# One pool of eight PSUM banks, finer words and a new order behind the fifth pair, in a Mamba-2 scan with a low-rank mixer

## The chip, the cores and the metric

The kernel runs on one core of one Trainium2 chip. The metric is device microseconds of one execution, the median over the runs. Engine names are those of the profile: PE is TensorE (PEld its weight loads), DVE is VectorE, ACT is ScalarE, POOL is GpSimd, SP is SyncE, which issues the DMAs here.

## What is computed

First a Mamba-2 scan over batch 4, 8 heads, 768 positions, head size 32 and state size 16, in chunks of 32; then a mixer on its output, laid out as x of shape (4, 768, 256):

```python
# scan, per chunk c, with cum = cumsum(log a) inside the chunk
L = exp(cum[:, None] - cum[None, :]) * causal
y = ((C B^T) * L) x + (C state) * exp(cum)[:, None]
state = exp(sum(la)) * state + sum_j exp(cum[-1] - cum[j]) * B_j x_j^T
# mixer, per batch; U is 768 x 32, V is 32 x 768
h = x.T @ U @ V
u = x + h.T
out = u + relu(u @ w_ch1) @ w_ch2          # w_ch1 256 x 1024, w_ch2 1024 x 256
```

The mixer's weights come as float64 and are taken apart into float32 on the chip.

## The kernel before, in words

**Order.** The whole program is one list of words, PLAN (L36), that `follow` (L862) walks through: each word calls one helper with the numbers behind it, and the helper issues its instructions at once. Tiles are placed and semaphores set for that order; each engine runs its own instructions strictly in the order of the words, and so does SP its DMAs. Nothing is reordered later.

**Scan words.** The 12 pairs k are 4 batches of 3 pieces of 256 positions; pair k holds 8 chunks. `P` (`prep`, L460) multiplies B and C by their decays on DVE; `T` (`turning`, L472, two words for one pair) transposes them on PE and copies them with ACT to T and Cm; `g` (`gram`, L507) makes four PSUM tiles of scores in 32-row tiles of PE; `m` and `M` (`mask`, L520) mask two of them each on DVE; `n` (`intra`, L629) multiplies them with x in 64 small matmuls into the two y tiles; `s` (`state`, L537) makes the two A tiles of new state in 32 small matmuls; `u` (`update`, L552) adds them to the running state, four dependent DVE instructions (three in the last pair of a batch) and one POOL product; `i` and `j` (`inter`, L602) add the state's part to y, `j` behind a POOL marker copy that waits for the matmuls of `i` and `n` (`apart`, L577); `y` (`yout`, L644) copies the two y tiles out with ACT; `t` (`ytokening`, L653) transposes that into token order and copies it with ACT (batches 0, 1) or DVE. `L`, `B`, `X`, `b`, `x` load a pair (L190 to L214, five DMAs in all).

**Mixer words**, with b the batch, j the half of its 768 positions, m one of 8 column blocks, k one of 3 output chunks of 128: `p`, `q`, `a` form u = x + h^T (`project`, `parted`, `added`, L677 to L703; `a` takes two PSUM tiles and two DVE adds). For batch 0 `U` (L739) and four `d` words per chunk use plain fp32. For the other batches each operand is split into a near part, a far part and their join, all in the faster fp32r form: `S` (`split`, L718) makes the three parts of u (ACT, then DVE twice), `f` (L750) four products of 384 columns and a scaling on ACT, `e` (L756) two more into the same bank and the near part on ACT, `h` (L764) the far part on DVE and, for odd m, the join of the pair (`joined`, L713). `d` (`down`, L773) has six words per chunk of four products of 256 columns: near, near, far, far, join, join, with an ACT scaling behind the fourth; the last one adds a product, DVE adds the token tile and SP sends 128 KB to the output.

**Weights.** `w`, `W`, `Z`, `z` load the float64 words; `c` (`convert`, L807, four steps each) makes fp32 of them with ACT and DVE, `R` (`refined`, L835) the three parts.

**PSUM.** `bank` (L143) gives a tile under a tag; the tags w, x, z, y have two banks each (L131). f and U use x and z in turn by m, g takes both of x and z, s both of w, transposes w, y tiles y; d takes x, z or y.

```python
    BANKS = {"w": 2, "x": 2, "z": 2, "y": 2}

    def bank(tag, *dims):
        t = psum.tile([P, *dims], FP32, tag=tag, name=tag, bufs=BANKS[tag])
        return t
```

Of the kernel before, what the change touches and what calls it, by code (L numbers as in the profile page):

```python
# [10 lines left out]
FP32 = mybir.dt.float32  # L11
# [12 lines left out]
ALU = mybir.AluOpType  # L24
# [10 lines left out]
    'b0.0 b0.1 b0.2 x0.0 x0.1 b1.0 b1.1 b1.2 ')  # L35
PLAN = (  # L36
# [37 lines left out]


@with_exitstack
def kernel(
# [27 lines left out]
    nc = tc.nc  # L105
    P = 128
    NB, NH, S, D = x.shape
# [11 lines left out]
    NQ = NM // 2  # L119
# [8 lines left out]
    psum = ctx.enter_context(  # L128
        tc.tile_pool(name="psum", bufs=1, space=bass.MemoryType.PSUM))

    BANKS = {"w": 2, "x": 2, "z": 2, "y": 2}  # L131

    def idle(t, n):

# [6 lines left out]
            n -= m  # L141

    def bank(tag, *dims):  # L143
        t = psum.tile([P, *dims], FP32, tag=tag, name=tag, bufs=BANKS[tag])
        return t

    ctx.enter_context(tc.manual_schedule())

    class Kept:
# [23 lines left out]
        out=a_sb,  # L173
# [11 lines left out]
    def begin(**kwargs):  # L185
        op = nc.sync.dma_start(**kwargs)
        if until:
            hold(op, until.pop())
# [32 lines left out]
    w1all = mix.tile([P, NQ, NCB, W], FP32, tag="u", name="w1f", bufs=1)  # L221
    w1f = [w1all[:, c] for c in range(NQ)]
    w2 = [const.tile([P, NM, DM], FP32R, name=f"w2{i}") for i in range(2)]
    weights = []
    w2f, w2b = {}, {}

    def w2c(n, dtype):
        return (w2f if dtype == FP32 else w2b).setdefault(n, mix.tile(
            [P, 2, DM], dtype, tag=f"w2c{n}", name=f"w2c{n}", bufs=1))


    def words_of(dst):
        p, i, j = dst.shape
        t = raw.tile([P, 2 * WCOLS], INT32, tag="words", name="words", bufs=NWORDS)
        weights.append((dst, t[:p, :2 * i * j]))
        return t[:p, :2 * i * j]

    def each(parts, *index):
        return [part[index] for part in parts]

    def load_words(dst, src):

        p, i, j = dst.shape
        t = words_of(dst)
        begin(out=t.rearrange("p (i j) -> p i j", i=i), in_=src)

    U2, V2, w12, w22 = (w.bitcast(INT32) for w in (moe_U, moe_V, moe_w_ch1, moe_w_ch2))
# [4 lines left out]

    def load_v():
        own["UV"] = words_of(UV)
        for q in range(4):
            begin(out=own["UV"][ts(q, Q), 2 * NC * RK:], in_=V2[:, ts(q, 2 * NC * RK)])

# [3 lines left out]

    def load_w(n):
        if n < 2:
            if n == 0:
                own["w"] = words_of(w1f[0])
                weights.pop()
            dst, t = w1f[0][:, :, ts(n, P)], own["w"][:, ts(n, 2 * NCB * P)]
            weights.append((dst, t))
            begin(out=t.rearrange("p (i j) -> p i j", i=NCB),
                  in_=w13[:, :, ts(n, 2 * P)])  # L270
        elif n <= NQ:
            load_words(w1f[n - 1], w13[:, :, ts(n - 1, 2 * quarter)])
        else:
            m = 2 * (n - NQ - 1)
            load_words(w2c(n - NQ - 1, FP32), w22[m * P:(m + 2) * P].rearrange(
                "(m p) d -> p m d", p=P))

    def load(k):
# [273 lines left out]
    def update(k, c=0, n=2):  # L552
# [7 lines left out]
        for i in own:  # L560
# [4 lines left out]
            else:  # L565
# [2 lines left out]
                    op0=ALU.mult, op1=ALU.add)  # L568
            st["S", b] = new
            st["Sm", b, j + 1] = s["Sm"][:, i].rearrange("p s d -> p (s d)")  # L570
        sl = slice(own[0], own[-1] + 1)
        nc.gpsimd.tensor_tensor(  # L572
            out=s["Sm"][:, sl], in0=s["S"][:, sl].rearrange("p i (s d) -> p i s d", s=2),
            in1=own2[:, b, 4 * q + sl.start:4 * q + sl.stop, :, None].to_broadcast(
                [P, len(own), 2, D]), op=ALU.mult)

    def apart(k):  # L577

# [62 lines left out]
                            stop=True, skip_group_check=True)  # L641
                        behind.setdefault(k, []).append(product)

    def yout(k):  # L644
        b, q = pairs[k]
        if q == 0 and b:
            yT[b] = mix.tile([P, NCB, S], FP32, tag="yT", name="yT")
            ytok[b] = mix.tile([P, NC, DM], FP32, tag="ytok", name="ytok")
        yp = yT[b][:, :, ts(q, 2 * P)].rearrange("p g (c v i) -> p g c v i", c=2, v=2)
        for p in range(2):  # L650
            nc.scalar.copy(out=yp[:, :, :, p], in_=st[k]["y"][p])  # L651

    def ytokening(k, tag="w"):  # L653

# [17 lines left out]
    def mixer(b):  # L672
# [91 lines left out]
        def third(j, m):  # L764

            near, far, both = gs[j, m // 2]
            vector.scalar_tensor_tensor(
                out=far[:, m % 2], in0=gs["t", j, m], scalar=0.0,
                in1=near[:, m % 2].bitcast(FP32), op0=ALU.max, op1=ALU.subtract)
            if m % 2:  # L770
                joined(near, far, both)

        def down(j, k, n):  # L773

# [18 lines left out]
            if n == pieces - 1:  # L793
# [3 lines left out]
                nc.sync.dma_start(out=out[b, ts(c, P)], in_=o)  # L797

        us, gs, gT = {}, {}, {}
        return SimpleNamespace(p=project, q=parted, a=added, S=split, f=first, e=second, h=third,  # L800
                               d=down, U=plain)


# [46 lines left out]
    def ytokens_kept(k):  # L850
        next(turns["O", k])

    scans = dict(P=prep, T=turned, g=gram, s=state, m=lambda k: mask(k, (0, 1)),
                 M=lambda k: mask(k, (2, 3)), u=update, i=lambda k: inter(k, 0), n=intra,
                 j=lambda k: inter(k, 1), y=yout, t=ytokens, L=load, Q=lambda k, c: prep(k, c, 1),
                 O=ytokens_of, o=ytokens_kept,
                 V=lambda k, c, v: turn(k, c, 1, "wx"[v // 2], vector if v % 2 else None))
# [54 lines left out]
```

## Time and profile before

| what | value |
|---|---|
| median of 3 runs | 225.08 us (224.58 to 226.39) |
| profiled execution, its own time | 225.03 us |
| its span, first to last instruction | 223.3 us |
| busy in the span: PE, DVE, ACT, POOL | 215.1, 156.7, 114.5, 14.7 us |
| mean granted TensorE clock | 1.00 |
| one state word on PE (L546, 32 matmuls) | 0.38 us |
| one `i` or `j` (L616, 16 matmuls), one `n` (L638, 64) | 0.43, 0.79 us |
| four f products of 384 columns (L728) | 0.70 us |
| one `d` word in fp32r, four products of 256 columns | 0.47 us |
| masks, two on DVE | 0.75 us |
| far part, join on DVE | 0.55, 0.96 us |
| state update on DVE, three instructions | 0.91 us |

Durations are those of the rows; where several instructions of a kind follow each other their sum over the row is used, since they overlap a little. The time outside the span is 1.7 us.

### The profile page before, as it was taken

The numbers are of one execution on the slowest core, as the hardware profiler recorded it, in microseconds if no ns is written. First come the engines' busy times: TensorE is split into PE (matmuls) and PEld (weight loads), VectorE is DVE, ScalarE is ACT, GpSimd is POOL, SyncE is SP. The second block draws the span as 40 slices with busy tenths as digits, with TensorE's granted clock in tenths as the row PEclk, the third lists the DMA queues.
The fourth block names the chain that finished last, engine by engine and source line by source line (L and its number), as shares of the span: only waits on it lengthen the run. The fifth ranks groups of instructions, "written<-read, shape, count | busy, mean of one in ns | idle before, by whom it ended". The sixth has DMA issues, their size and how long they took to land.

```text
span 223.3 us, 7012 instructions
## 1 busy us (share of the span) xinstructions
PE 215.1 (96%) x3012; PEld 181.6 (81%) x3012; DVE 156.7 (70%) x330; ACT 114.5 (51%) x261; POOL 14.7 (7%) x37
## 2 busy tenths in 40 slices
PE   7989799999999999999999999999999999999993
PEld 4657565556678998987999898897998999999993
DVE  4786689899998857879627784849437965764921
ACT  2336766766993365425354533375237545655410
POOL 3021020013100000203001000100000000000000
PEclk9999999999999999999999999999999999999999
DMA  6987599777737014300003402000020000100111
GB/s 94 133 121 160 110 172 288 110 209 171 98 51 97 26 44 59 64 23 26 3 26 62 83 0 73 3 3 3 1 73 0 0 8 18 47 0 28 35 36 47
DMA packets 69518, 14.56 MB, mean 65 GB/s; under 512 B 63792, under 2 KB 67696, under 8 KB 69488
## 3 DMA queue, kind: packets, MB, share of 16 engines
q1 hardware_dynamic: 69488, 14.13, 31.8%
q8 instruction: 23, 0.38, 0.8%
q14 instruction: 7, 0.06, 0.1%
HBM read 10.98 MB, written 3.15 MB: 63 GB/s over the span
## 4 chain that ended last, share of the span: by engine, by line
PE 90%; DVE 4%; issue 2%; ACT 1%; DMA 1%; POOL 0%; DVEq 0%; POOLq 0%; ACTq 0%
PE x L728 31%; PE z L728 24%; PE y L728 12%; PE y L616 4%; PE y L638 4%; PE x L514 3%; PE w L483 3%; PE w L659 2%; PE w L546 2%; PE z L514 2%; PE w L682 1%; DMA a_sb<-in_a_dram 1%; DVE words L160 1%; PE w L138 1%; DVE S L160 1%
## 5 line engine op out<-in xcount | busy, mean ns | idle before, releaser
L160 DVE SCALAR_TENSOR_TENSOR words<-words 128x768 fp32r<-128x768 f32 (+6 forms) x44 | 34.6, 806 | 1.9 <-ACT words L419 0.6
L728 PE MATMUL z<-u,w 128*128 128x384 f32 x144 | 34.2, 351 | 0.0
L728 PE MATMUL x<-u,w 128*128 128x384 f32 x144 | 33.2, 347 | 0.0
L733 ACT ACTIVATE x<-x 128x384 f32<-128x384 f32 (+1 forms) x30 | 13.6, 452 | 25.1 <-PE x L728 24.1
L728 PEld LDWEIGHTS z<-u,w 128*128 128x128 f32 x144 | 24.5, 188 | 1.5 <-DVE words L160 0.2
L728 PEld LDWEIGHTS x<-u,w 128*128 128x128 f32 x144 | 24.0, 188 | 1.2 <-ACT x L733 0.6
L160 DVE SCALAR_TENSOR_TENSOR words<-x,words 128x384 fp32r<-128x384 f32 x24 | 13.2, 555 | 16.3 <-ACT words L762 13.6
L728 PE MATMUL x<-w2c,words 128*128 128x256 f32 x112 | 22.5, 338 | 0.0
L733 ACT ACTIVATE z<-z 128x384 f32<-128x384 f32 (+1 forms) x27 | 12.5, 463 | 14.2 <-PE z L728 13.8
L728 PEld LDWEIGHTS x<-w2c,words 128*128 128x128 f32 x112 | 18.3, 189 | 1.3
L728 PE MATMUL y<-w,words 128*128 128x256 f32 x144 | 18.9, 280 | 0.0
L728 PEld LDWEIGHTS y<-w,words 128*128 128x128 f32 x144 | 18.3, 188 | 0.4 <-DVE ytok L160 0.4
L160 DVE SCALAR_TENSOR_TENSOR words<-z,words 128x384 fp32r<-128x384 f32 x24 | 13.3, 552 | 5.6 <-ACT words L762 5.6
L762 ACT ACTIVATE words<-x 128x384 fp32r<-128x384 f32 x24 | 11.7, 490 | 6.3 <-PE x L728 6.2
L762 ACT ACTIVATE words<-z 128x384 fp32r<-128x384 f32 x24 | 11.6, 491 | 4.9 <-PE z L728 4.8
L651 ACT COPY yT<-y 128x256 f32<-128x256 f32 x24 | 7.9, 385 | 11.1 <-PE y L616 10.9
L572 POOL TENSOR_TENSOR Sm<-S,own 128x256 f32<-128x256 f32 (+1 forms) x12 | 7.7, 646 | 86.4 <-DVE S L160 57.0
L160 DVE SCALAR_TENSOR_TENSOR S<-S,kept,w 128x64 f32<-128x64 f32 x40 | 11.2, 280 | 2.7 <-PE w L546 1.0
L728 PE MATMUL x<-w,words 128*128 128x256 f32 x96 | 12.5, 281 | 0.0
L616 PE MATMUL y<-T,Sm 32*64 32x64 f32 x352 | 12.1, 239 | 0.3 <-POOL Sm L572 0.3
L638 PE MATMUL y<-M,x 64*32 64x64 f32 x768 | 11.0, 224 | 1.1 <-issue 1.0
L728 PEld LDWEIGHTS x<-w,words 128*128 128x128 f32 x96 | 11.9, 189 | 0.1
(153 smaller groups left out, 399.4 us busy)
## 6 DMA issues: line engine op xcount, KB each, us to landing
words<-in_moe_w_ch_dram SPq DMA_DIRECT2D x7, 512.0 KB, 6.4
x<-in_x_dram SPq DMA_DIRECT2D x24, 128.0 KB, 3.3
out_dram<-ytok SPq DMA_DIRECT2D x24, 128.0 KB, 1.7
bc<-in_B_dram SPq DMA_DIRECT2D x24, 64.0 KB, 3.1
bc<-in_C_dram SPq DMA_DIRECT2D x12, 128.0 KB, 3.1
words<-in_moe_w_ch_dram SPq DMA_DIRECT2D x2, 256.0 KB, 4.7
words<-in_moe_V_dram SPq DMA_DIRECT2D x4, 48.0 KB, 2.4
words<-in_moe_U_dram SPq DMA_DIRECT2D x1, 192.0 KB, 4.7
```

The source lines that it names most:

```text
L160: self.last = call(*args, **kwargs)
L483: nc.tensor.transpose(out=tp[:, i, v], in_=s["BC"][:, i, c + v].rearrange("p h n -> p (h n)"), identity=ident)
L514: nc.tensor.matmul(out=g[r][cols, c], lhsT=s["T"][rows, 0, c, cols], rhs=s["Cm"][rows, :, :, ts(2 * c + p, Q)].rearrange("r v t i -> r v i ...
L546: nc.tensor.matmul(out=s["A"][p][ts(r, Q), v], lhsT=s["BC"][half, 0, v, 2 * r:2 * r + 2].rearrange("p h n -> p (h n)"), rhs=x_sb[k][half, ...
L572: nc.gpsimd.tensor_tensor(out=s["Sm"][:, sl], in0=s["S"][:, sl].rearrange("p i (s d) -> p i s d", s=2), in1=own2[:, b, 4 * q + sl.start:4 ...
L616: product = nc.tensor.matmul(out=y[p][ts(r % 2, H), r // 2, c], lhsT=own[ts(r, Q)], rhs=s["T"][ts(r, Q), 1, :, ts(2 * c + p, Q)].rearrange ...
L638: product = nc.tensor.matmul(out=y[p][ts(i, Q), n, c], lhsT=x_sb[k][half, c, h], rhs=s["M"][half, h // 2, c, h % 2], start=fresh(k, p, [i] ...
L651: nc.scalar.copy(out=yp[:, :, :, p], in_=st[k]["y"][p])
L659: nc.tensor.transpose(out=t[:, c, g], in_=yT[b][:, g, ts(2 * q + c, P)], identity=ident)
L728: nc.tensor.matmul(out=t, lhsT=lhsT, rhs=rhs, start=start, stop=True, skip_group_check=True)
L733: nc.scalar.activation(t, t, AF.Copy, scale=1.0 + EPS)
L762: nc.scalar.activation(gs[j, m // 2][0][:, m % 2], t, AF.Relu, scale=NEAR)
```

## The change

Three things change. PSUM's eight banks become one pool under one tag, so that any tile takes any free bank; the names passed to `bank` stay as names only. The words u and y are cut in two (`u` by half pair, with the POOL product behind the second half; `y` by tile), and the join gets a word of its own, `J` (`fourth`), in place of a call inside `h`; the list of loaded weights becomes a dictionary, so that loads may come in another order. Behind u5 all words stand in a new order; in front of it the order is the same but for the cut words. Apart from the cut words and J both plans hold the same words.

Of the two plans, the lines that the text speaks of:

```diff
-    'x2.0 x2.1 b3.1 b3.2 W0 Z0 V2.0.2 V2.1.3 n1 i1 s2 g2 z0 x3.1 x3.0 W1 b4.0 j1 y1 P3 u2 m2 M2 T3 '
...
-    'w7 w8 U0.0.3 P6 U0.0.2 c6 U0.0.6 s5 c4 c4 U0.1.7 c6 U0.1.2 u5 R0 R2 U0.1.6 n4 s6 L7 i4 g5 c6 '
...
-    'd1.1.0.5 d1.1.2.4 d1.1.2.5 d1.1.1.4 d1.1.1.5 T10 g9 m9 T10 T11 T11 M9 i9 n9 g10 m10 M10 j9 y9 '
-    's11 u11 i10 g11 m11 M11 n10 f2.0.4 a2.1 f2.0.3 f2.0.2 e2.0.4 h2.0.4 e2.0.3 e2.0.2 f2.0.7 '
...
-    'e2.1.6 d2.1.0.0 e2.1.7 d2.1.2.0 d2.1.2.1 d2.1.2.2 h2.1.6 h2.1.7 d2.1.2.3 a3.0 S3.0 d2.1.0.1 '
...
-    'd3.1.0.2 d3.1.0.3 d3.1.2.4 d3.1.2.5 d3.1.0.4 d3.1.0.5 ')
+    'F1.0 j0 y0.0 y0.1 x2.0 x2.1 b3.1 b3.2 W0 Z0 V2.0.2 V2.1.3 n1 i1 s2 g2 z0 x3.1 x3.0 W1 b4.0 j1 '
+    'y1.0 y1.1 P3 u2.0 u2.1 m2 M2 T3 T3 O0.0 i2 c0 c1 c1 n2 g3 M3 c1 c1 j2 y2.0 y2.1 m3 t1 O2.1 s3 '
...
+    'c4 U0.1.7 c6 U0.1.2 u5.0 u5.1 R0 L8 T6 c7 U0.1.6 c7 U0.1.5 c7 i4 R3 g5 n4 m5 c6 T6 U0.0.5 M5 c8 '
+    'L7 c8 U0.0.4 c8 c9 c7 U0.1.4 U0.0.7 c9 c9 n5 c6 i5 j4 R5 P8 y4.1 y4.0 P7 g6 j5 m6 L10 y5.1 t4 '
+    'd0.1.0.0 T8 y5.0 d0.1.0.1 T8 c8 T7 T7 c9 M6 d0.1.0.2 d0.1.0.3 R1 R2 s6 n6 s7 s8 u6.0 u6.1 u7.0 '
+    't5 u7.1 u8.0 R2 u8.1 d0.1.1.0 R1 d0.1.1.1 R4 d0.1.1.2 d0.1.1.3 i6 g7 m7 L11 M7 p1 j6 g8 R3 P10 '
+    'q1 d0.0.0.0 R6 d0.0.0.1 R7 M8 a1.0 d0.0.2.0 d0.0.1.0 d0.0.1.1 d0.0.0.2 R5 d0.0.2.1 y6.0 S1.0 m8 '
...
+    'e1.0.6 h1.0.2 e1.0.0 n7 n8 h1.0.0 i7 i8 h1.0.1 T10 S1.1 d0.1.2.0 d0.1.2.1 R4 j7 y7.1 J1.0.0 j8 '
+    'T10 d0.1.2.2 y8.0 h1.0.6 L9 f1.1.1 f1.1.5 d0.1.2.3 f1.1.3 y7.0 e1.1.1 R4 f1.1.0 d1.0.0.0 f1.1.2 '
+    'e1.1.0 h1.1.1 d0.0.1.3 R7 e1.1.2 d1.0.0.1 e1.1.5 d1.0.1.0 R6 y8.1 f1.1.4 h1.1.2 P9 d1.0.2.0 '
...
+    'h1.1.6 e1.1.7 p2 s10 h1.1.7 s9 T9 u9.0 u9.1 d1.0.1.3 u10.0 q2 d1.1.1.0 u10.1 d1.0.1.4 J1.1.0 '
...
+    'e2.0.3 h2.0.3 f2.0.4 d1.1.1.4 d1.1.1.5 a2.1 d1.1.2.4 d1.1.2.5 e2.0.1 d1.1.0.4 h2.0.7 h2.0.1 g9 '
+    'M9 m9 T11 e2.0.4 d1.1.0.5 h2.0.4 g10 M10 T11 m10 f2.0.2 s11 n9 u11.0 i9 u11.1 g11 e2.0.2 m11 '
+    'f2.0.0 j9 M11 i10 y9.0 y9.1 i11 n11 n10 f2.0.6 f2.0.5 e2.0.0 e2.0.6 h2.0.2 j10 j11 y11.1 J2.0.1 '
...
+    'h2.1.7 h2.1.3 d2.0.2.5 e2.1.5 S3.0 d2.1.2.0 d2.0.1.5 d2.0.0.4 d2.1.2.1 d2.1.1.0 f3.0.1 f3.0.4 '
...
+    'd3.1.1.3 J3.1.2 d3.1.2.2 d3.1.2.3 d3.0.1.5 d3.1.0.4 d3.1.1.4 d3.0.0.4 d3.1.0.5 d3.1.2.4 '
+    'd3.1.1.5 d3.1.2.5 d3.0.0.5 d3.0.2.4 d3.0.2.5 ')
```

Of the helpers:

```diff
     psum = ctx.enter_context(
         tc.tile_pool(name="psum", bufs=1, space=bass.MemoryType.PSUM))
-    BANKS = {"w": 2, "x": 2, "z": 2, "y": 2}
+    BANKS = 8
     def idle(t, n):
...
             n -= m
     def bank(tag, *dims):
-        t = psum.tile([P, *dims], FP32, tag=tag, name=tag, bufs=BANKS[tag])
-        return t
+        return psum.tile([P, *dims], FP32, tag="bank", name=tag, bufs=BANKS)
     ctx.enter_context(tc.manual_schedule())
...
     w1all = mix.tile([P, NQ, NCB, W], FP32, tag="u", name="w1f", bufs=1)
     w1f = [w1all[:, c] for c in range(NQ)]
     w2 = [const.tile([P, NM, DM], FP32R, name=f"w2{i}") for i in range(2)]
-    weights = []
+    weights = {}
     w2f, w2b = {}, {}
     def w2c(n, dtype):
...
     def words_of(dst):
         p, i, j = dst.shape
         t = raw.tile([P, 2 * WCOLS], INT32, tag="words", name="words", bufs=NWORDS)
-        weights.append((dst, t[:p, :2 * i * j]))
         return t[:p, :2 * i * j]
     def each(parts, *index):
         return [part[index] for part in parts]
-    def load_words(dst, src):
+    def load_words(n, dst, src):
         p, i, j = dst.shape
         t = words_of(dst)
+        weights[n] = dst, t
         begin(out=t.rearrange("p (i j) -> p i j", i=i), in_=src)
     U2, V2, w12, w22 = (w.bitcast(INT32) for w in (moe_U, moe_V, moe_w_ch1, moe_w_ch2))
...
     def load_v():
         own["UV"] = words_of(UV)
+        weights[1] = UV, own["UV"]
         for q in range(4):
             begin(out=own["UV"][ts(q, Q), 2 * NC * RK:], in_=V2[:, ts(q, 2 * NC * RK)])
...
     def load_w(n):
         if n < 2:
-            if n == 0:
+            if "w" not in own:
                 own["w"] = words_of(w1f[0])
-                weights.pop()
             dst, t = w1f[0][:, :, ts(n, P)], own["w"][:, ts(n, 2 * NCB * P)]
-            weights.append((dst, t))
+            weights[2 * n] = dst, t
             begin(out=t.rearrange("p (i j) -> p i j", i=NCB),
                   in_=w13[:, :, ts(n, 2 * P)])
         elif n <= NQ:
-            load_words(w1f[n - 1], w13[:, :, ts(n - 1, 2 * quarter)])
+            load_words(n + 1, w1f[n - 1], w13[:, :, ts(n - 1, 2 * quarter)])
         else:
             m = 2 * (n - NQ - 1)
-            load_words(w2c(n - NQ - 1, FP32), w22[m * P:(m + 2) * P].rearrange(
+            load_words(n + 1, w2c(n - NQ - 1, FP32), w22[m * P:(m + 2) * P].rearrange(
                 "(m p) d -> p m d", p=P))
     def load(k):
...
                     op0=ALU.mult, op1=ALU.add)
             st["S", b] = new
             st["Sm", b, j + 1] = s["Sm"][:, i].rearrange("p s d -> p (s d)")
-        sl = slice(own[0], own[-1] + 1)
+        if c + n < 2:
+            return
+        sl = slice(0, own[-1] + 1)
         nc.gpsimd.tensor_tensor(
             out=s["Sm"][:, sl], in0=s["S"][:, sl].rearrange("p i (s d) -> p i s d", s=2),
-            in1=own2[:, b, 4 * q + sl.start:4 * q + sl.stop, :, None].to_broadcast(
-                [P, len(own), 2, D]), op=ALU.mult)
+            in1=own2[:, b, 4 * q:4 * q + sl.stop, :, None].to_broadcast(
+                [P, sl.stop, 2, D]), op=ALU.mult)
     def apart(k):
...
                             stop=True, skip_group_check=True)
                         behind.setdefault(k, []).append(product)
-    def yout(k):
+    def yout(k, p):
         b, q = pairs[k]
-        if q == 0 and b:
+        if b not in yT:
             yT[b] = mix.tile([P, NCB, S], FP32, tag="yT", name="yT")
             ytok[b] = mix.tile([P, NC, DM], FP32, tag="ytok", name="ytok")
         yp = yT[b][:, :, ts(q, 2 * P)].rearrange("p g (c v i) -> p g c v i", c=2, v=2)
-        for p in range(2):
-            nc.scalar.copy(out=yp[:, :, :, p], in_=st[k]["y"][p])
+        nc.scalar.copy(out=yp[:, :, :, p], in_=st[k]["y"][p])
     def ytokening(k, tag="w"):
...
             vector.scalar_tensor_tensor(
                 out=far[:, m % 2], in0=gs["t", j, m], scalar=0.0,
                 in1=near[:, m % 2].bitcast(FP32), op0=ALU.max, op1=ALU.subtract)
-            if m % 2:
-                joined(near, far, both)
+
+        def fourth(j, n):
+
+            joined(*gs[j, n])
         def down(j, k, n):
...
                 nc.sync.dma_start(out=out[b, ts(c, P)], in_=o)
         us, gs, gT = {}, {}, {}
-        return SimpleNamespace(p=project, q=parted, a=added, S=split, f=first, e=second, h=third,
+        return SimpleNamespace(p=project, q=parted, a=added, S=split, f=first, e=second, h=third, J=fourth,
                                d=down, U=plain)
...
         next(turns["O", k])
     scans = dict(P=prep, T=turned, g=gram, s=state, m=lambda k: mask(k, (0, 1)),
-                 M=lambda k: mask(k, (2, 3)), u=update, i=lambda k: inter(k, 0), n=intra,
+                 M=lambda k: mask(k, (2, 3)), u=lambda k, c: update(k, c, 1), i=lambda k: inter(k, 0), n=intra,
                  j=lambda k: inter(k, 1), y=yout, t=ytokens, L=load, Q=lambda k, c: prep(k, c, 1),
                  O=ytokens_of, o=ytokens_kept,
                  V=lambda k, c, v: turn(k, c, 1, "wx"[v // 2], vector if v % 2 else None))
```

52 rows, old and new, of the table PLAN are left out of this document.

## The prediction, made before the changed kernel ran

> **What bounds the kernel now.** I read the page's busy shares and chain first, then the table by stretch, then the chain in order of time, then the timeline around single waits.
>
> ```profile
> PE 215.1 (96%) x3012; PEld 181.6 (81%) x3012; DVE 156.7 (70%) x330; ACT 114.5 (51%) x261; POOL 14.7 (7%) x37
> ...
> PEclk9999999999999999999999999999999999999999
> ...
> PE 90%; DVE 4%; issue 2%; ACT 1%; DMA 1%; POOL 0%; DVEq 0%; POOLq 0%; ACTq 0%
> ```
>
> PE is busy for 96% of the span and is 90% of the chain, at the full granted clock in every slice. By stretch (columns: stretch, then busy time and instructions of PE, PEld, DVE, ACT, POOL, then clock, DMA share and GB/s):
>
> ```profile
> 20.00:30.00 10.00, 8.69 (x313) 5.89 (x301) 7.80 (x24) 7.37 (x21) 1.36 (x3) 1.00 0.79 128
> 50.30:67.20 16.90, 16.82 (x454) 11.71 (x453) 16.29 (x37) 14.66 (x32) 2.36 (x4) 1.00 0.58 104
> 136.00:144.00 8.00, 8.00 (x301) 6.41 (x300) 5.43 (x16) 3.19 (x8) 0.88 (x3) 1.00 0.12 37
> 175.00:219.50 44.50, 44.46 (x328) 43.85 (x326) 27.27 (x45) 20.42 (x46) 0.00 (x0) 1.00 0.06 22
> 219.50:223.30 3.80, 0.15 (x2) 0.00 (x0) 0.42 (x1) 0.00 (x0) 0.00 (x0) 1.00 0.20 69
> ```
>
> The fifth pair's update u5 is done at 50.3 us, so the reordered part is the last 173 us, and PE has no visible hole there. What can be won is hidden inside PE's busy time, as pieces that are longer than their like. The chain in order of time shows them (start, length, what):
>
> ```profile
> 114.78 0.38 PE w L546 x32
> 137.28 0.80 PE w L483 x6
> 140.29 0.55 PE w L546 x20
> 143.13 0.90 PE x L728 x4
> 144.37 0.79 PE z L728 x4
> 149.17 0.70 PE z L728 x4
> 151.05 0.43 PE y L616 x16
> ```
>
> Four products of 384 columns take 0.70, a whole state word (L546, 32 matmuls) 0.38; 20 of them taking 0.55 is a wait, and 0.90 for the first four large products behind small ones is the price of changing kind. Against their own usual spacing the matmul starts after 50.3 are late by: 0.15 at 53.9 (T6's bank waits for u6), 0.24 at 70.2 (second bank of a0.1), 0.18 in s7 at 101.4, 0.08 at 105, 0.3 in g9 around 136.5, 0.3 in 140 to 142, 0.2 at 210.2, and about nine waits of 0.09 on a ScalarE copy of f or e. Sum 2.2 us. That is all that a better order can take from waits.
>
> **The change, part by part.** The sum is made against the profiled execution: 225.03 us, span 223.3, 1.7 around it; the median of the runs is 225.08.
>
> *Splits.* u, y and the join J are own words; both plans hold the same words otherwise, so PE keeps 3012 matmuls, DVE 330 and ACT 261 instructions, POOL one product of 0.65 us per pair. Cost 0.
>
> *Direct chains.* I counted, for each word, PE's work between it and what it needs. A product e needs f's ScalarE scaling: 0.28 for the last matmul to come out, 0.475 for the copy, about 0.1 between engines, 0.87 in all; in the old order 7 of 48 have less (0.69, one f between), in the new one none (shortest 0.87). Of near before d (0.28 + 0.49 + 0.1 = 0.87) five had 0.47, now at least 0.94. g9 to n9 (four masks, 1.98) had 1.22, now 3.6. S3.0 (1.1 of adds, 0.84, 0.96, together 3.5 with the ends) had 2.82 in front of f3.0.1, now 4.56. All 21 short places go, and the waits on the old pairs of banks (53.9, 70.2, 101.4, 140) have other banks to take: -2.2, bounds -2.2 and 0. What is late next is the queue of DVE, in the pool part below.
>
> *Kinds.* PE passes from small-tile words (g, i, j, n, s, p) to another kind 56 times behind u5, in the new order 43 times, since s7 s8, n7 n8, i7 i8, i10 i11 and others now stand together; each passage costs about 0.1 (0.15 from the last L546 start to the next large one, 0.01 to 0.04 inside). That is -1.3. Passages between transposes and large products rise from 13 to 26 at some 0.06 each: +0.8. Sum -0.5, bounds -1.3 and 0.
>
> *The pool.* A tile takes the bank that was freed longest ago in the order of the words. With eight live at the peak, that can be one read just before. Followed through the new order, four allocations hang on the queue of DVE. (a) d0.0.2.0 takes the bank that M8 reads last. From the end of d0.1.0.3 DVE has u6, u7, u8 (11 x 0.30), R2, R1, R3 (1.3 each), M7, m7, M8 (0.75 each), P10 0.68, q1 0.43 and two adds of 0.42, 11.4 us, and some 0.7 for the first latency and the wait for g7; PE has 11.8. Late by 0.3. (b) d1.1.1.0 behind u9: 0.2. (c) g9's fourth bank is d1.1.2's, whose add ends 1.1 after d1.1.2.5, with 0.82 of PE work between: 0.3. (d) g10 behind M9 and m9: 0.3. Sum +1.1. If every DVE time were exact and the small words ran slower, 0; with DVE another 0.7 behind, 1.0 at each, 4.0. I take 1.1, from the rows that the sum was made of.
>
> *The part in front of u5* keeps its order, but T3 now takes the bank of y1.0. The timeline shows T3's transposes and the copies of y1:
>
> ```profile
> 20.45 0.66 PE L483 MATMUL w<-ident,BC 128*128 128x128 f32 x4
> 20.59 0.65 ACT L651 COPY yT<-y 128x256 f32<-128x256 f32 x2 [2.09 <-PE y L616]
> 22.40 0.60 ACT L664 COPY ytok<-x 128x512 f32<-128x512 f32 x1
> 23.61 0.45 PE L638 MATMUL y<-M,x 64*32 64x64 f32 x28 [1.01 <-issue]
> ```
>
> The first copy ends at 20.97, so T3 starts 0.55 later. The hole of 1.01 us at 22.6, in which PE waits for none of the engines, may take that up: between 0 and +0.55, I take +0.2. Other early banks change owner, but not to a later reader.
>
> *Queues.* L8 now comes before L7, and L9 after L10 and L11. Each issues five transfers, 2.7 us of SP, and its B and C rows land about 4 us after the first issue (85.78 to 89.70 for L9). From L9's place to P9 there are 9 us of PE work, from L7 to P7 almost 6: cost 0, and 1 to 2 us if that cover went. R, c and J stand elsewhere on ACT and DVE; DVE's work per 10 us of PE work is at most 11. POOL's three products behind u6 to u8 end about 2 us before j6's marker copy needs POOL. At the end four outputs follow in 2.2 us; SP takes 0.33 to 0.38 for each and they land after 1.7, so the tail of 3.8 us stays (0 to +0.4).
>
> *The clock.* The order of before has short idle moments between groups of matmuls all along (1.0 at 22.6, some 0.1 at each change of kind), and the granted clock is 1.00 in every slice. The Trainium skill says, in TensorE: Matmul & The Clock Gate, section A second HAM failure mode: psum-queue depth-cycling, that cycling through the banks with frequent short idle moments can make the clock gate fall back and degrade the throughput. By that rule, which this trace does not bear out, a rotation over all eight banks would speak against the change. From rows alone: one stretch of small tiles such as 136 to 144, 8 us long, at half clock would cost 8 us; that is the last rival.
>
> Sum: 225.03 - 2.2 - 0.5 + 1.1 + 0.2 = 223.6 us.
>
> **The rivals.** *More gain.* The four pool waits and T3's are hidden: 225.03 - 2.7 = 222.3. For it: every direct chain has room. Against: M8 ends with no room.
>
> *Slower than before: DVE falls behind.* From T10 over S1.1 to S2.0 PE has about 30 us and DVE, by my count, ends 1.1 to 1.6 us behind it around p2, s9 and u9; t6's copy, u9 and the adds of a2.0 stand in one queue, and d1.1.1.0, a2.0 and f2.0.7 wait for it. Each 0.1 us that DVE loses there beyond that goes to PE. At 15% more on 20 us of DVE work it is +3: 223.6 + 3 = 226.6; it outweighs the gain from +1.4 on. For it: the page's mean of one instruction is some 7% above the spacing that I used. Against: the old order carries queues as long on DVE (9.03 of 10 us busy in 30 to 40, 16.29 of 16.9 behind u5) without a hole in PE.
>
> *It does nothing.* Waits move one for one: 225.0. For it: PE is 96% busy. Against: the 21 short chains are gone.
>
> *The clock falls back*: 223.6 + 8 = 231.6. Against: clock 1.00 in all slices.
>
> **How the numbers follow.** About 1% is what a measurement of this kernel can tell from no change: 222.8 and 227.3 are the edges. Forecast 0.42, with its own range of 222.7 to 224.4; more gain 0.28 (221.3 to 222.8); nothing 0.13 (224.4 to 225.5); DVE behind 0.15 (225.5 to 229); clock 0.02. Faster by over 1%: 0.28 and 0.02 of the forecast's edge, 0.30. Slower by over 1%: 0.10 of DVE behind and 0.02, 0.12. Within 1%: 0.58. Range for 8 in 10: 221.5 to 226.6; it leaves out about 0.05 below and 0.14 above.
>
> **What would show it.** Right: PE's busy share stays near 96%, pieces of four large products stay at 0.70 behind 50 us, no L546 or L514 word is stretched, and the end moves by 1 to 2 us. The pool waits would show as PE or PEld waiting for DVE M, S or ytok at d0.0.2.0, d1.1.1.0, g9 and g10, T3's as PE waiting for ACT yT near 21. Wrong: a PE hole over 0.5 us behind u5, a clock below 1.00, P9 waiting for its rows, or PE pieces longer than 0.70 with nobody to wait for.

## The result, and the profile after

The changed kernel takes 222.0 us (median of 4 runs, 221.59 to 222.47) against 224.83 for the kernel before (4 runs, 224.35 to 226.39): a ratio of 0.9877, 95% interval 0.9839 to 0.9916. Run again beside the experiments it gave 0.9907 (0.987 to 0.9944). The profiled execution took 222.37 us with a span of 220.7; that of before 225.03 and 223.3. The forecast was 223.6, with 222.7 to 224.4 as its own range; the time came out below that, where the rival "more gain" stood (222.3).

The page of after, same lines as those of before: busy time of PE to POOL, the clock, the chain by engine.

```profile
PE 211.9 (96%) x3012; PEld 181.1 (82%) x3012; DVE 154.5 (70%) x330; ACT 114.3 (52%) x261; POOL 15.5 (7%) x37
...
PEclk9999999999999999999999999999999999999999
...
PE 86%; DVE 6%; ACT 3%; issue 2%; DMA 1%; POOL 0%; DVEq 0%; ACTq 0%; POOLq 0%
```

PE does the same 3012 matmuls at the same clock in 3.2 us less. The chain now runs over DVE and ACT for 9% where it was 5%: a sign of new waits, to which we come. By stretch (PE, PEld, DVE, ACT, POOL, then clock, DMA share and GB/s):

```profile
20.00:30.00 10.00, 8.49 (x307) 5.89 (x291) 8.29 (x27) 7.19 (x20) 1.32 (x3) 1.00 0.76 126
50.10:67.00 16.90, 16.76 (x309) 11.63 (x308) 15.25 (x32) 12.37 (x28) 1.97 (x3) 1.00 0.70 127
139.60:152.60 13.00, 13.00 (x439) 11.06 (x438) 8.50 (x22) 6.02 (x15) 1.01 (x4) 1.00 0.08 25
172.00:216.90 44.90, 44.90 (x333) 44.61 (x331) 26.56 (x44) 19.46 (x44) 0.00 (x0) 1.00 0.08 29
216.90:220.70 3.80, 0.11 (x1) 0.00 (x0) 0.42 (x1) 0.00 (x0) 0.00 (x0) 0.97 0.25 87
```

Again there is no hole behind 50 us, and the tail is 3.8 us as before. So the 2.6 us of span lie inside PE's busy time. To find them I took from each trace the stretch from the first matmul behind U0.1.2 (the last word of PE ahead of u5) to the start of the kernel's last product. It holds the same matmuls in all kernels here, and it repeats well: 166.62 and 166.61 in two executions of the changed kernel, 165.40 and 165.48 in two of the one called "four waits mended" below. What lies ahead of it does not repeat: that first matmul starts at 50.19 in before, at 50.11 in after, and between 49.73 and 51.23 in seven other executions, whose words ahead of u5 are the same. The profiled executions of three more runs (pool alone, the mended kernel again, one stretch less) were slow ones that lost 3.4 to 4.9 us there, so of them only what lies behind u5 is read.

| us from the first matmul behind U0.1.2 to the start of the last product | in all | small-tile words g, i, j, n, s | transposes | large products, a and q with them |
|---|---|---|---|---|
| before | 169.18 | 20.95 | 6.53 | 139.33 |
| after | 166.62 | 18.46 | 5.85 | 139.95 |
| cut words alone | 169.12 | 20.97 | 6.53 | 139.26 |
| pool alone | 168.59 | 20.48 | 6.44 | 139.30 |
| joined words apart | 168.29 | 19.27 | 6.04 | 140.62 |
| short chains put back | 168.15 | 18.66 | 5.85 | 141.28 |
| turns of T joined, five | 168.24 | 18.90 | 5.84 | 141.13 |
| turns of T joined, three | 167.32 | 18.89 | 5.90 | 140.18 |
| four waits mended | 165.40 | 18.46 | 5.79 | 138.78 |
| mended, one stretch less | 167.44 | 20.47 | 5.82 | 138.79 |

(Each matmul is counted up to the start of the next; the projections p, 2.36 in all kernels, make up the rest.) All of the 2.56 us comes from the small words and the transposes; the large products even got 0.6 longer, since a wait is counted to the matmul ahead of it and 1.2 us of new waits, which the mended kernel below takes away again, stand behind large products. The chain of after shows how the small words got shorter (start, length, what):

```profile
146.84 0.97 PE y L620 x44
147.81 1.41 PE y L642 x91
149.22 0.90 PE x L731 x4
150.12 0.70 PE z L731 x4
...
151.51 0.71 PE y L620 x32
```

Two n words (L642) take 1.41 together, alone 0.79 each; two j words (L620) 0.71 together, alone 0.43 each. A stretch is a run of small-tile words with nothing else between them on PE; it pays once for the way in and out (the 0.90 of the four products behind it, where 0.70 is usual). Counted so, projections among them, there are 16 behind u5 in before and 13 in after (the expectation below says 17).

Inside a stretch a change of the tile's size costs too. The words n and s use tiles of 64 rows, g, i and j tiles of 32. Inside a word the next matmul usually starts 0.007 us after the last. From n to i or j it takes 0.146, from i or j to n or s 0.158, from g to n 0.225; from n to s, of one size, 0.01 to 0.03. These spacings are the same in before and after. Before has 15 such changes inside its stretches (those to and from p counted), after 8: 2.46 us against 1.45. So of the 2.49 us that the small words lost, 1.0 are these changes, 0.6 lie at the ends of the stretches (0.2 of it waits behind j4 and j7), and 0.9 are waits inside words, such as 0.35 in g9, that are gone.

The new waits are in the list of what PEld waited for behind 50 us (total, times, longest):

```profile
PEld z L731 <- issue: 0.5, 1, 0.5
...
PEld w L485 <- DVE M L162: 0.5, 1, 0.5
...
PEld z L703 <- DVE M L162: 0.3, 1, 0.3
...
PEld y L731 <- ACT words L765: 0.2, 1, 0.2
```

In the order of the list: f1.1.1 at 103.4 (first product 0.41 late, behind the read of f1.0.6's tile by h1.0.6), T8 at 64.4 (0.31, behind m6), the second tile of a1.0 at 79.7 with d0.0.2.0 next to it (0.34, behind M8), d3.1.2.1 at 205.2 (0.25, for the near part of e3.1.4). The first shows in the timeline:

```profile
101.89 0.96 DVE L162 SCALAR_TENSOR_TENSOR words<-words 128x768 fp32r<-128x768 f32 x1 [0.70 <-ACT w L447]
...
102.77 0.55 DVE L162 SCALAR_TENSOR_TENSOR words<-x,words 128x384 fp32r<-128x384 f32 x1
...
103.47 1.28 PE L731 MATMUL z<-u,w 128*128 128x384 f32 x6 [0.18 <-DVE words L162]
```

J1.0.0 (0.96) stands ahead of h1.0.6 (0.55) on DVE, and f1.1.1 gets the bank that h1.0.6 reads.

### The profile page after: what moved, and what is told of

Its sections match the earlier page's. It is cut to its first block, busy times and chain, and to the rows that moved or that the text cites. A ratio compares the mean times of both kernels' runs of the same rounds, so it can differ in the third digit from the quotient of the medians.

```text
span 220.7 us, 7036 instructions
## 1 busy us (share of the span) xinstructions
PE 211.9 (96%) x3012; PEld 181.1 (82%) x3012; DVE 154.5 (70%) x330; ACT 114.3 (52%) x261; POOL 15.5 (7%) x37
## 4 chain that ended last, share of the span: by engine, by line
PE 86%; DVE 6%; ACT 3%; issue 2%; DMA 1%; POOL 0%; DVEq 0%; ACTq 0%; POOLq 0%
PE x L731 29%; PE z L731 24%; PE y L731 12%; PE y L642 3%; PE y L620 2%; PE x L516 2%; PE w L485 2%; DVE words L162 2%; PE w L548 2%; PE w L662 2%; PE z L516 1%; PE w L685 1%; DVE M L162 1%; DVE BC L162 1%; PE w L693 1%
## 5 line engine op out<-in xcount | busy, mean ns | idle before, releaser
L162 DVE SCALAR_TENSOR_TENSOR words<-words 128x768 fp32r<-128x768 f32 (+6 forms) x44 | 33.8, 801 | 2.7 <-ACT words L421 1.0
L731 PE MATMUL z<-u,w 128*128 128x384 f32 x144 | 32.1, 340 | 0.2 <-DVE words L162 0.2
L731 PE MATMUL y<-w,words 128*128 128x256 f32 x144 | 20.3, 281 | 0.0
L731 PEld LDWEIGHTS y<-w,words 128*128 128x128 f32 x144 | 19.3, 189 | 0.2 <-ACT words L765 0.2
L576 POOL TENSOR_TENSOR Sm<-S,own 128x256 f32<-128x256 f32 (+1 forms) x12 | 8.6, 721 | 81.8 <-DVE S L162 63.1
L731 PE MATMUL x<-w,words 128*128 128x256 f32 x96 | 14.1, 284 | 0.0
L731 PEld LDWEIGHTS x<-w,words 128*128 128x128 f32 x96 | 12.8, 188 | 0.3 <-issue 0.2
L731 PE MATMUL z<-yT,w1f 128*128 128x384 f32 x32 | 11.8, 496 | 0.0
L731 PE MATMUL x<-yT,w1f 128*128 128x384 f32 x32 | 11.4, 489 | 0.1
L447 ACT ACTIVATE w<-words 128x512 fp32r<-128x512 f32 x8 | 5.0, 628 | 12.5 <-DVE words L162 12.5
```

The lines of the kernel that those rows point to most:

```text
L162: self.last = call(*args, **kwargs)
L447: nc.scalar.activation(low, far, AF.Copy, scale=1.0 / EPS)
L576: nc.gpsimd.tensor_tensor(out=s["Sm"][:, sl], in0=s["S"][:, sl].rearrange("p i (s d) -> p i s d", s=2), in1=own2[:, b, 4 * q:4 * q + sl.st ...
L731: nc.tensor.matmul(out=t, lhsT=lhsT, rhs=rhs, start=start, stop=True, skip_group_check=True)
```

## The experiments

Two theories went in. *Stretches and waits*: the order gains by fewer stretches of small words and by chains without waits, and loses some of it to new waits on DVE. *Pool*: the freedom of eight banks brings the gain. A third, the price of my forecast, was that each passage between transposes and large products costs 0.06. All ratios are to the kernel before, of runs on one chip; the differences under 1% are read from the table above.

**The changed kernel again** (no edit).

> The changed kernel once more, to have it beside the others on one chip. Every theory: 222.0 us, a ratio of 0.988 to the kernel before.

222.35 us, ratio 0.9907 (0.987 to 0.9944).

**Cut words alone.** before's order, u, y and J cut in place, four pairs of banks:

```diff
-u4 w6 w7 w8
+u4.0 u4.1 w6 w7 w8
...
-h1.0.1 e1.0.6
+h1.0.1 J1.0.0 e1.0.6
...
-j4 y4 u6 T6
+j4 y4.0 y4.1 u6.0 u6.1 T6
```

> The cut words alone: u, y and J cut, the parts side by side, in the order of before and with its four pairs of banks. Every theory: no change, a ratio of 1.00 to the kernel before (224.8 us); the one thing that could move it is the one POOL product per pair, issued behind the second half of the update, at most 0.2 us.

224.6 us, ratio 0.9981 (0.9949 to 1.0012); behind u5 0.06 less. The cuts cost and gain nothing.

**Pool alone**: the same plan with `BANKS = 8`.

> The pool of eight banks and the cut words alone, in the order of before (u, y and J cut, the parts standing side by side). First theory, fewer islands: what the change gained is mainly that small-tile words behind u5 stand together, 13 stretches of them on PE where there were 17, and each stretch less saves about 0.33 us. The pool alone then takes only the waits on the old pairs of banks (0.15 at 53.9, up to 0.24 at 70.2, 0.18 at 101.4, some 0.2 in 140 to 142): 225.0 - 0.7 = 224.3 us. Rival, the pool: a free bank always at hand is what brought the gain, and the order adds little: 222.5 us.

224.28 us, ratio 0.9986 (0.9959 to 1.0013); behind u5 169.18 - 168.59 = 0.59 less, 0.7 had been expected. It is a net: g9 is 0.35 shorter, and other old waits go, but new ones come, the longest, 0.51, at f2.0.4, where the trace names nothing that PE waits for. So the pool by itself is a quarter of what the change gained, and "pool" falls. The order alone, on four pairs of banks, wasn't tried: it holds y7 and y8 open together, four tiles where the tag has two banks.

**Joined words apart**:

```diff
-d0.0.1.2 e1.0.6 h1.0.2 e1.0.0 n7 n8 h1.0.0 i7 i8 h1.0.1
+d0.0.1.2 n7 e1.0.6 h1.0.2 i7 e1.0.0 n8 i8 h1.0.0 h1.0.1
-j7 y7.1 J1.0.0 j8 T10 d0.1.2.2 y8.0
+j7 y7.1 J1.0.0 T10 d0.1.2.2 j8 y8.0
-i11 n11 n10 f2.0.6 f2.0.5
+i11 n11 f2.0.6 n10 f2.0.5
-j10 j11 y11.1 J2.0.1 h2.0.0 t9 e2.0.5
+j10 J2.0.1 h2.0.0 t9 e2.0.5 j11 y11.1
```

> The changed kernel with five of its joined small-tile words pulled apart by large products: n7 and i7 from n8 and i8, j7 from j8, n10 from n11, j10 from j11. Fewer islands: each place brings one more stretch, with 0.09 to enter it from large products and some 0.25 to leave it, 0.33 in all: 222.0 + 1.65 = 223.7 us. Rival, waits: the gain came from waits on copies and banks alone, and standing together is worth nothing: 222.0 us, at most 222.3.

223.86 us, ratio 0.9957 (0.9933 to 0.9982). Behind u5 168.29 - 166.62 = 1.67 more for five stretches more: 0.33 each, as expected. The number of changes of tile size inside stretches is 8 in both, so this is the price of a stretch alone. In its timeline n7 and i7 stand among products:

```profile
96.10 0.86 PE L642 MATMUL y<-M,x 64*32 64x64 f32 x64
96.89 0.62 PE L731 MATMUL x<-u,w 128*128 128x384 f32 x2
97.43 0.50 PE L620 MATMUL y<-T,Sm 32*64 32x64 f32 x16
97.86 0.61 PE L731 MATMUL x<-u,w 128*128 128x384 f32 x2
```

The two e words between (x2) take 0.54 from start to start, and 0.35 where they stand among large products.

**Short chains put back**: seven e words moved forward to one f behind their own f, for instance

```diff
-f1.0.4 y6.1 f1.0.3 R6 d0.0.2.3 f1.0.7 e1.0.4
+f1.0.4 y6.1 f1.0.3 e1.0.4 R6 d0.0.2.3 f1.0.7
```

> The changed kernel with seven short chains of the old order put back: e1.0.4, e1.1.1, e2.0.7, e2.0.6, e3.0.4, e3.1.1 and e2.1.2 stand one f (0.70 us of PE work) behind their own f, where 0.87 is needed. First theory, the chains are waits on the path: each costs the 0.09 to 0.18 that the trace of before and the sum of latencies give, 222.0 + 0.6 to 1.2, so 222.9 us; in the trace the fifth to sixth product of such a pair starts late behind a ScalarE copy. Rival: PE runs on from a queue of its own, or other waits behind take it up, and nothing is seen: 222.0 us.

224.35 us, ratio 0.9936 (0.9906 to 0.9967); behind u5 1.53 more. Of this 1.15 lies at the seven chains, 0.11 to 0.26 each and 0.16 in the mean: a first product that starts late, and 0.11 more because the product behind it starts late too (0.28 behind the first, where 0.175 is usual). The rest lies mainly at e2.0.3 (0.33), which has the moved e2.0.7 no longer in front of it and so became an eighth short chain, and in n11 (0.20, cause not shown). PEld waits for the copies again, as it did in before; after has no such line. Of this kernel, behind 50 us:

```profile
PEld x L731 <- ACT x L736: 1.0, 4, 0.3
PEld z L731 <- ACT z L736: 0.9, 4, 0.4
```

Of the kernel before:

```profile
PEld x L728 <- ACT x L733: 0.6, 3, 0.2
...
PEld z L728 <- ACT z L733: 0.2, 1, 0.2
```

The ratio moves less than the trace does against the changed kernel's 0.9907, which was measured on another chip; the intervals are too wide to tell that apart.

**Turns of T joined**: T6, T8, T9, T10, T11, each two words apart in after, stand together.

> The changed kernel with the two halves of T6, T8, T9, T10 and T11 standing together again, five stretches of transposes less between large products. By the trace of after, a stretch of transposes between large products costs nothing (the step into it 0.003, the step out of it -0.08 and +0.085): 222.0 us, at most 0.1 from it. Rival, the price of the forecast: 10 passages less at 0.06 each, 222.0 - 0.6 = 221.4 us.

223.85 us, ratio 0.9962 (0.9929 to 0.9995); behind u5 1.62 more than after, which neither expected. PE waits 1.62 us at f1.1.5 alone. That the two numbers agree is chance: 0.4 each at d1.1.1.0 and g11 come on top, and three of the waits of after (f1.1.1, T8, d3.1.2.1) are gone. The wait at f1.1.5:

```profile
104.68 0.80 PE L731 MATMUL z<-u,w 128*128 128x384 f32 x3 [1.46 <-ACT yT L654]
```

f1.1.5 takes the bank of a y7 tile, in this kernel as in after, and the copy of that tile is late. What ACT did, in this kernel:

```profile
99.06 0.59 ACT L489 COPY T<-w 128x512 f32<-128x512 f32 x1 [2.19 <-PE w L485]
99.54 0.84 ACT L495 ACTIVATE Cm<-w,slot 128x256 f32<-128x256 f32 x2
100.27 0.85 ACT L726 ACTIVATE u<-yT 128x768 fp32r<-128x768 f32 x1
103.74 0.63 ACT L447 ACTIVATE w<-words 128x512 fp32r<-128x512 f32 x1 [2.62 <-DVE words L162]
104.27 0.35 ACT L654 COPY yT<-y 128x256 f32<-128x256 f32 x1
```

and in after:

```profile
97.57 0.85 ACT L726 ACTIVATE u<-yT 128x768 fp32r<-128x768 f32 x1
101.23 0.63 ACT L447 ACTIVATE w<-words 128x512 fp32r<-128x512 f32 x1 [2.81 <-DVE words L162]
101.81 0.37 ACT L654 COPY yT<-y 128x256 f32<-128x256 f32 x1
```

With T10's second word ahead of S1.1, T10's three copies (1.43) come ahead of S1.1's near part (L726) on ACT; the far part and the join of u on DVE come later by as much, then R4's part (L447), then y7.1's copy, then PE. Without T10 and T8:

> The changed kernel with the halves of T6, T9 and T11 standing together, T8 and T10 left apart: the run before this one had the halves of T10 together too, and there f1.1.5 got a bank that a copy of y8 reads late, and PE waited 1.62 us for it. Transposes beside large products free: 222.0 us, at most 0.15 from it, the span of the profiled execution within 0.15 of 220.7. Rival, the price of the forecast: six passages less at 0.06 each, 222.0 - 0.36 = 221.6 us, a span of 220.3. Other rival, the pool: with T6 and T9 moved, banks behind them change hands again, and a new wait of 0.3 or more stands somewhere behind 55.

223.98 us, ratio 0.9931 (0.9901 to 0.9961), a span of 222.5; of the 1.8 over after 1.1 lie ahead of u5 and 0.70 behind it. Against after, the words between T6's two places stand 0.22 earlier and those behind them even, around T9 0.18 to 0.36 earlier, even again behind the wait at a2.0 and then 0.22 later, around T11 0.22 later and then 0.20 earlier: of the turns themselves at most 0.03 is left. The 0.70 is mainly a wait of 0.43 in g11 and one of 0.26 at a2.0. The first has the same cause as the 1.62: T11's copies now stand ahead of e2.0.4's near part on ACT,

```profile
142.38 0.59 ACT L489 COPY T<-w 128x512 f32<-128x512 f32 x1 [1.29 <-PE w L485]
142.86 0.85 ACT L495 ACTIVATE Cm<-w,slot 128x256 f32<-128x256 f32 x2
143.59 0.51 ACT L765 ACTIVATE words<-x 128x384 fp32r<-128x384 f32 x1
```

so h2.0.4, M10, m10 and u11 are late on DVE, and g11's last tile has the bank that u11 reads. The second stands behind DVE's part of q2, which waits its turn behind u9 and the first half of u10. So the passages are free, as the first theory had it, and a wait appeared, as the last rival had it, but not because banks changed hands (f1.1.5 kept its bank): my reading of the 1.62 in the expectation, that another bank had been dealt, was wrong as well. What a turn that moves changes is the place of its copies on ACT.

**Four waits mended**:

```diff
-h1.0.1 T10 ... y8.0 h1.0.6 L9
+h1.0.1 h1.0.6 T10 ... y8.0 L9
-g8 R3 P10 q1 d0.0.0.0 R6 d0.0.0.1 R7 M8 a1.0
+g8 R3 M8 q1 P10 d0.0.0.0 R6 d0.0.0.1 R7 a1.0
-P8 y4.1 y4.0 P7 g6 j5 m6 L10
+P8 y4.1 y4.0 g6 j5 m6 P7 L10
-d3.0.1.4 h3.1.4 d3.1.2.1 d3.0.2.3
+d3.0.1.4 h3.1.4 d3.0.2.3 d3.1.2.1
```

> The changed kernel with the four places mended at which its trace shows PE waiting behind u5 for another engine: h1.0.6 before T10 in place of behind y8.0 (f1.1.1 waits 0.41 for its read), M8 before q1 and P10 (a1.0 and d0.0.2.0 wait 0.34 for it), P7 behind m6 (T8 waits 0.31 for m6), d3.1.2.1 behind d3.0.2.3 (waits 0.25 for the copy of e3.1.4). If these are waits on the path: 222.0 - 1.3 = 220.7 us. Rival, the slack is only moved: DVE is as late as before and the next allocation waits in its place, 221.8 us.

221.24 us, ratio 0.9857 (0.9821 to 0.9893), the fastest so far; behind u5 1.22 less than after, 1.3 had been expected. The four lines are gone from its list, and its chain is PE's again:

```profile
PE 91%; DVE 4%; ACT 1%; issue 1%; DMA 1%; POOL 0%; DVEq 0%; ACTq 0%; POOLq 0%
```

Once more, on another chip: 221.45 us, ratio 0.9835 (0.9791 to 0.9879).

> The kernel with the four mended waits once more, to have it beside the next: 221.2 us, a ratio of 0.985.

**Mended, one stretch less**:

```diff
-g9 M9 m9 T11 e2.0.4 d1.1.0.5 h2.0.4 g10 M10 T11 m10 f2.0.2 s11 n9 u11.0 i9 u11.1 g11 e2.0.2 m11
-f2.0.0 j9 M11 i10 y9.0 y9.1 i11 n11 n10 f2.0.6 f2.0.5 e2.0.0 e2.0.6 h2.0.2 j10 j11
+g9 M9 m9 T11 T11 e2.0.4 d1.1.0.5 h2.0.4 g10 M10 s11 n9 i9 m10 f2.0.2 u11.0 u11.1 f2.0.0 e2.0.2
+g11 h2.0.2 M11 m11 j9 i10 n10 y9.0 y9.1 i11 n11 f2.0.6 f2.0.5 e2.0.0 e2.0.6 j10 j11
```

> The mended kernel with one stretch of small-tile words less: g10, s11, n9 and i9 stand together, f2.0.2, f2.0.0 and e2.0.2 behind them, and g11 stands with j9, i10, n10, i11 and n11; both halves of T11 stand behind g9. Fewer islands: 0.33 for the stretch less, 221.2 - 0.3 = 220.9 us. Rival: g10, s11 and y9 fill the eight banks, so f2.0.2, and y10 behind g11, wait for DVE's masks by as much, 221.2 us or more.

223.0 us, ratio 0.9911 (0.9874 to 0.9948); behind u5 2.04 more than the mended kernel. Of this 0.52 lies at g5, at 58 us, where both have the same words: a bank comes free late, since ACT waited 0.98 for weights to land before it could copy it out. That is no effect of the edit. The other 1.5 is, and the medians agree (223.0 against 221.45 of the runs beside it). The rival was right, and too mild: n9 and i10 wait for DVE to free their banks.

```profile
PEld y L642 <- DVE words L162: 0.4, 1, 0.4
PEld y L620 <- DVE words L162: 0.3, 1, 0.3
```

These two and what follows them make the small words 1.5 us longer. A join pays 0.33 only while banks are free for it.

## Why the prediction was right in sign and short in size

The forecast's sum was -2.2 - 0.5 + 1.1 + 0.2 = -1.4 us; the span moved by -2.6. Step by step:

- *Splits, 0.* Right: 169.12 against 169.18.
- *Waits of the old order, -2.2.* Right in kind and about right in size. In the trace of before, the matmuls behind u5 that start later than their like elsewhere are late by about 2.4 in all: 1.1 behind copies of f, e and near (0.79 of it at seven places of f and e, where the forecast had nine of 0.09), 1.1 in the small words and behind j4 and j7, and 0.2 around T6. The list holds two slips. The word at 101.4 is s9, not s7. The 0.24 at 70.2 is no wait: the first product of a1.1, fp32r behind plain fp32, takes 0.40 where 0.17 is usual, but the plain product ahead of it takes 0.09 where 0.32 is usual, and with eight banks it is the same. In its place 0.19 behind T6, at 54.8, was not on the list.
- *Kinds, -1.3 for the small words.* Right in kind, too small. The count of 13 passages less holds, but each is worth 0.15, not 0.1: three stretches less at about 0.33 make -1.0, and seven changes of tile size less inside stretches make another -1.0. The first price was tested by an edit (joined words apart); the second is read from the spacing of matmuls alone, which is the same in every trace here.
- *Kinds, +0.8 for transposes beside large products.* This step failed. 13 stretches of transposes became 18 behind u5, and they cost nothing:

```profile
157.07 0.71 PE z L731 x4
157.78 0.44 PE w L662 x4
158.22 0.47 PE x L731 x4
```

  Four transposes take 0.44, their own 0.11 each, and the products around them 0.71 and 0.47, as always. I had read an excess of 0.08 on the first product behind transposes as a cost, and overlooked that the last transpose is as much shorter.
- *The pool, +1.1.* The sum was right (1.22 by the mended kernel) by luck: of the four places only one bore out in full. M8 makes the tiles beside and behind a1.0 wait 0.34 (0.3 forecast). d1.1.1.0 starts some 0.08 late behind u9 (0.2 forecast). g9 and g10 have the banks that I named, but DVE had read them in time. The others were f1.1.1, T8 and d3.1.2.1; the last is no bank at all but a chain. DVE was on time where I thought it late, and late behind one J of 0.96 that I had not looked at.
- *T3, +0.2.* Wrong. In the built program T3's tile lies in a bank of s2, not in that of y1.0: the banks do not go around simply in the order of the words. The timeline has T3 ahead of y1's copies:

```profile
20.50 0.66 PE L485 MATMUL w<-ident,BC 128*128 128x128 f32 x4
...
20.64 0.65 ACT L654 COPY yT<-y 128x256 f32<-128x256 f32 x2 [2.10 <-PE y L620]
```

  With the hole at 22.6, now 0.66 on issue, and other small things, the part ahead of u5 is 0.08 shorter, far less than the 1.5 by which it varies from one execution to another.
- *Queues, tail.* Right, no cost: P9 waits for no rows, and the tail is 3.8 us.
- *DVE falls behind* did not come: behind 50 us PE is busy for at least 9.8 of every 10 us. *The clock falls back* did not come: the clock is 1.00 in every stretch until PE's work ends, and 0.97 only in the tail. The rotation over all eight banks did not show what the Trainium skill says in TensorE: Matmul & The Clock Gate, section A second HAM failure mode: psum-queue depth-cycling. *More gain* gave the right time for the wrong reason: its pool waits were not hidden; the small words saved more than forecast and the transposes were free.

With the measured terms the sum is -2.4 for the old waits, -2.0 for the small words, +1.2 for the four new waits and -0.1 in front. Two small terms nobody had foreseen come to about +0.4: 0.15 of new waits that were not mended (d1.1.1.0 and e2.0.3), and some 0.2 by which the products of 256 columns take longer in after, 0.0006 each, which no trace here explains. That makes -2.9, where the span moved by -2.6; so the old waits, which no edit put back as a whole, are known to no better than 0.3.

## What to carry to other kernels

On a saturated PE count what the tiles cost at their borders: here a stretch of small tiles among large products cost 0.33 us, a change of tile size inside it 0.14 to 0.22, a stretch of transposes nothing. A chain that is too short costs its late start and 0.11 more at the product behind; put one back to see its price, and look whether the move shortens another chain. And one pool for all tiles is worth little by itself; it lets the order move, and then every word moved on PE takes its copies along on the other engines: before moving one, look at what stands behind them there. Where two traces are compared, see first that the difference stands where the edit is: 0.5 us of one comparison here came from a load that landed late.

## What the runs showed of the hardware

- Transposes (128x128, fp32) between products of 256 and 384 columns: 0.11 us each and no cost for the change, over 10 passages to fp32r products and 8 to plain fp32 ones in after.
- The first fp32r product behind a plain fp32 one takes 0.36 instead of 0.17, but the last plain one takes 0.19 less; the change of precision costs nothing.
- From one tile size to another the next small matmul starts 0.146 (64 rows to 32), 0.158 (32 to 64, behind i or j) or 0.225 us (behind g) after the last, where 0.007 is usual inside a word; into a stretch it is 0.09 more than the large product's own time, and the first large fp32r product of 384 columns behind it takes 0.28 where 0.175 is usual.
- The time behind U0.1.2 repeated to 0.01 us in the changed kernel and to 0.07 in the mended one; what did not repeat lay in the first 50 us (1.5 us between nine executions, 3.4 to 4.9 more in three others), except for the 0.5 at g5.
